# Lightning attention with a bilinear FFN: one kv update in another slot, one scaling on GpSimd, three idle matmuls out

## The chip, the cores and the metric

One core of a Trainium2 chip. The metric is the device time of one execution in microseconds (us); the profile of one execution comes with it, and its span is some 2 us shorter than the device time.

## The reference

Linear attention over blocks with a decay per head, then an FFN whose hidden layer is a product of two projections. Cut to what matters:

```python
for b in range(nb):                       # blocks of the sequence, per batch and head
    intra = einsum(qb, kb) * Dmask        # scores within the block, causal, decayed
    out   = intra @ vb + (qb * lam_pow) @ kv_state
    kv_state = lam_block * kv_state + einsum(kb * rev_pow, vb)
x = out as [B*S, H*D]
result = ((x @ w_a) * (x @ w_b)) @ w_out
```

B, H, S, D are 4, 8, 768, 64. The FFN is 512 to 1536 and back to 512. Inputs and output are f32; the result may carry bf16 error.

## The kernel before

The kernel works in 24 units of 128 tokens, six for each batch. The FFN runs over groups of 4, 1, 2, 4, 4, 4, 4 and 1 units. While TensorE works on the FFN of one group, "hooks" slip in the attention pieces of later units. A table says which piece is recorded at which slot. Each engine executes its own instructions in the order in which they are recorded, and so does the sync engine, from whose queue nearly all transfers are issued.

```python
PLAN = {
    ...
    1: [(0, "V", 4), (2, "T", 5), (3, "PK", 6), (6, "PV", 6), ...],
    2: [(0, "V", 6), (1, "T", 7), (1, "P", 8), (4, "T", 8), (5, "P", 9), (6, "S", 7),
        (6, "S", 8), (7, "V", 7), (8, "P", 10), (10, "T", 9), (11, "T", 10),
        (12, "Q", (7, 8, 9, 10)), (12, "P", 11), (13, "V", 9), (14, "P", 12), ...],
    3: [(3, "S", 11), (3, "S", 12)],
}
for _g, _u in ((3, 11), (4, 15), (5, 19)):
    PLAN.setdefault(_g, []).extend(
        [(1, "P", _u + 2), (3, "P", _u + 3), (4, "V", _u),
         (7, "Q", (_u, _u + 1, _u + 2, _u + 3)), ...])
```

P prepares a unit: q and k are scaled by powers of the decay into `qk` (its half PK), v is cast to `vb`, and loads of later units are issued (its half PV). T transposes q and k on TensorE. From unit 11 on there is no T: a DMA transpose does it, issued as soon as q and k are scaled. S makes scores and masks. V makes the kv update and its copy to SBUF. Q makes the outputs of two units and the scores of the next two.

```python
    def prep_k(u):
        early = u < n0 + 3                               # n0 = 4
        make_ks(u, "dve" if early else "pool")
        make_qs(u, "pool")
        used["u"] = u + 1
        if u >= DMA_T_FROM:                              # 11
            ...
            nc.sync.dma_start_transpose(out=qkT..., in_=U[u]["qk"]...)

    def prep_v(u):
        make_vb(u, "pool" if u < n0 + 3 else "dve")
        pump()                                           # loads up to unit used + 2

    def pieces_O(us, nxt=()):                            # pieces O, O2 and Q
        kqs = [score_banks() for u in nxt]
        for u in us:
            inter(u)                                     # needs the state of unit u - 1
        for u, kq in zip(nxt, kqs):
            scores(u, kq)
        for u in us:
            intra(u)
            evac_o(u, ...)
        if len(us) == 2 and us[0] >= n0 + 3:
            kv_beside(us[1])                             # eight 64-column matmuls
        for u, kq in zip(nxt, kqs):
            masks(u, kq)                                 # two VectorE ops per unit
        if len(us) == 2 and us[0] >= n0 + 3 and us[1] % NB < NB - 1:
            kv_copy(us[1], kv["ps"])

    # head
    for at, i, j in ((2, 0, 0), (3, 0, 1), (4, 1, 0)):
        scale4("k", i, j)
        part_k(i, j, at)
        warm(3)                                          # three idle matmuls of 128 columns
    scale4("k", 1, 1)
```

Of the kernel before, what the change touches and what calls it, by code (L numbers as in the profile page):

```python
# [22 lines left out]
def _bc(ap, dims):  # L23
# [20 lines left out]
    1: [(0, "V", 4), (2, "T", 5), (3, "PK", 6), (6, "PV", 6), (6, "S", 5), (7, "T", 6),  # L44
        (10, "S", 6), (12, "O2", (5, 6)), (13, "P", 7)],
    2: [(0, "V", 6), (1, "T", 7), (1, "P", 8), (4, "T", 8), (5, "P", 9), (6, "S", 7),
        (6, "S", 8), (7, "V", 7), (8, "P", 10), (10, "T", 9), (11, "T", 10),
        (12, "Q", (7, 8, 9, 10)), (12, "P", 11), (13, "V", 9), (14, "P", 12),
        (14, "O2", (9, 10))],
    3: [(3, "S", 11), (3, "S", 12)],  # L50
# [12 lines left out]
def kernel(  # L63
# [12 lines left out]
    B, H, S, D = q.shape  # L76
    BLK = 128
    NB = S // BLK
# [89 lines left out]
    n0 = GROUPS[0]  # L168
# [24 lines left out]
    def warm(n, cols=128):  # L193
        for _ in range(n):
            nc.tensor.matmul(idle_ps[:, :cols], lhsT=idle_sb[:, :128], rhs=idle_sb[:, :cols],  # L195
                             start=True, stop=True, skip_group_check=True)
# [55 lines left out]
    def eng_of(name):  # L252
        return nc.gpsimd if name == "pool" else nc.vector

    def make_ks(u, eng):
        qk = prep_pool.tile([128, 2, H, D], BF16, name="qk", tag="qk")
        eng_of(eng).tensor_mul(qk[:, 1], raw.pop((u, "k")),  # L257
                               lp_k[:, u % NB].to_broadcast([128, H, D]))
        U[u] = dict(qk=qk, kn=qk[:, 1])

    def make_qs(u, eng):
        eng_of(eng).tensor_mul(U[u]["qk"][:, 0], raw.pop((u, "q")),  # L262
                               lp_q[:, u % NB].to_broadcast([128, H, D]))
# [8 lines left out]
        U[u]["vb"] = vb  # L272

    def prep_k(u):
        early = u < n0 + 3
        make_ks(u, "dve" if early else "pool")
        make_qs(u, "pool")
        used["u"] = u + 1
        if u >= DMA_T_FROM:
            qkT = qkT_pool.tile([128, 2, HP, 128], BF16, name="qkT", tag="qkT")  # L280
            nc.sync.dma_start_transpose(
                out=qkT[:].rearrange("p j hp i -> p (j hp) i"),
                in_=U[u]["qk"][:].rearrange("p j h d -> p (j h d)"))
            U[u]["qT"], U[u]["kT"] = qkT[:, 0], qkT[:, 1]
# [15 lines left out]
    def score_banks():  # L300
        return [ps_bank(f"kq{i}", [128, HP, 128], F32) for i in range(2)]

    def scores(u, kq=None):
        d = U[u]
        kq = kq or score_banks()
        for hp in range(HP):
            for i in range(2):
                p = slice(64 * i, 64 * i + 64)
                nc.tensor.matmul(kq[i][:, hp, :], lhsT=d["kT"][p, hp, :], rhs=d["qT"][p, hp, :],  # L309
                                 start=True, stop=True, skip_group_check=True)  # L310
        return kq

    def masks(u, kq):
        ms = mask(kq)
        U[u]["m"] = lambda i, hp: ms[i][:, hp, :]
# [15 lines left out]
    def inter(u):  # L331
        d = U[u]
        if u % NB > 0:
            first = o_bank(u)
            for hp in range(HP):
                nc.tensor.matmul(d["o"][:, hp, :], lhsT=st_bufs[(u - 1) % 4][:, hp, :, :],  # L336
                                 rhs=d["qT"][:, hp, :], start=(first and hp == 0), stop=True,
                                 skip_group_check=True)

    def intra(u, first=False):  # L340
        d = U[u]
        first = o_bank(u) or first
        for hp in range(HP):
            for i in range(2):
                p = slice(64 * i, 64 * i + 64)
                nc.tensor.matmul(d["o"][p, hp, :], lhsT=d["vb"][:, 2 * hp + i, :],  # L346
                                 rhs=d["m"](i, hp), start=(first and hp == 0),
                                 stop=True, skip_group_check=True)

    def evac_o(u, xT, col, eng="act"):  # L350
        o_ps = U[u].pop("o")
        if eng == "act":
            nc.scalar.copy(xT[:, :, col:col + BLK], o_ps)  # L353
        else:
            nc.vector.tensor_copy(xT[:, :, col:col + BLK], o_ps)
# [19 lines left out]
    def kv_beside(u):  # L375
        if u % NB == 0 or u % NB == NB - 1:
            kv_update(u)
        for hp in range(HP if 0 < u % NB < NB - 1 else 0):
            for i in range(2):
                p = slice(64 * i, 64 * i + 64)  # L380
                nc.tensor.matmul(kv["ps"][p, hp, i, :], lhsT=U[u]["kn"][:, 2 * hp + i, :],
                                 rhs=U[u]["vb"][:, 2 * hp + i, :],
                                 start=False, stop=True, skip_group_check=True)

    def kv_copy(u, ps, eng="dve"):
        st = st_bufs[u % 4]
        if eng == "act":
            for i in range(2):
                p = slice(64 * i, 64 * i + 64)
                nc.scalar.copy(st[p, :, i, :], ps[p, :, i, :])  # L390
        else:
            nc.vector.tensor_mul(st[:].rearrange("p hp i d -> p hp (i d)"),  # L392
                                 ps[:].rearrange("p hp i d -> p hp (i d)"), bdiag_bc)
# [11 lines left out]
    def pieces_O(us, nxt=()):  # L405
        kqs = [score_banks() for u in nxt]
        for u in us:
            inter(u)
# [3 lines that stand above are left out]
            intra(u)  # L412
            xT, col = xTs[u]
            evac_o(u, xT, col)
        if len(us) == 2 and us[0] >= n0 + 3:
            kv_beside(us[1])
        for u, kq in zip(nxt, kqs):
            masks(u, kq)
        if len(us) == 2 and us[0] >= n0 + 3 and us[1] % NB < NB - 1:
            kv_copy(us[1], kv["ps"])  # L420


# [89 lines left out]
    def scale4(w, i, j):  # L512
        hs = slice(4 * i + 2 * j, 4 * i + 2 * j + 2)
        nc.vector.tensor_mul(
            xs4[w].rearrange("p r (h d) -> p h r d", d=D)[:, hs],
            x4[w, i][:, :, 2 * j:2 * j + 2].rearrange("p r h d -> p h r d"),
            (lp_q if w == "q" else lp_k)[:, NB:, hs, :].rearrange("p r h o -> p h r o")
            .to_broadcast([128, 2, PACK, D]))
        if j == 1:
            staged.pop((w + "4", i))  # L520
# [9 lines left out]
    def part_k(i, j, at):  # L530
        tps = packed_bank("k", at)
        transpose4("k", i, j, tps)
        unpack(i, tps, slice(j, j + 1), "k")
# [45 lines left out]
    for at, i, j in ((2, 0, 0), (3, 0, 1), (4, 1, 0)):  # L579
        scale4("k", i, j)  # L580
        part_k(i, j, at)
        warm(3)
    scale4("k", 1, 1)
    for u in range(n0):
        make_vb(u, "pool")
# [39 lines left out]
    for g, n in enumerate(GROUPS):  # L625
# [6 lines left out]
        def hook(slot, plan=plan):  # L632
            for name, us in plan.get(slot, ()):
                if name == "C":
                    cast_w("o", us, "dve")
                elif name == "PK":
                    prep_k(us)
                elif name == "PV":
                    prep_v(us)
                elif name == "P":  # L640
                    prep_k(us)
                    prep_v(us)
                elif name == "T":
                    piece_T(us)
                elif name == "S":
                    piece_S(us)
                elif name == "V":
                    piece_V(us)
                elif name == "O":
                    pieces_O((us,))  # L650
                elif name == "O2":
                    pieces_O(us)
                else:
                    pieces_O(us[:2], us[2:])
# [31 lines left out]
```

## Time and profile before

| | before |
|---|---|
| device time, median of the first three executions | 236.69 us (236.5 to 237.27) |
| the profiled execution | 236.32 us, span 234.5 us |
| TensorE busy | 226.2 us |

The prediction shows the lines that carry the argument. In the timeline, the columns are start, duration, engine, source line, operation, tiles and shapes; brackets give the engine's idle time just before and what ended it. In the chain of waits, a piece has start, duration and what ran or was waited for. In a list of waits, the figures are total us, number of waits and the longest. The tile names: `a_ps` and `b_ps` are the two projections, `ab` their product, `op` the output projection, `kq` scores, `m` masked scores, `o_ps` attention output, `kvd` and `st` the state in PSUM and SBUF, `tps` and `qkT` transposed q and k.

The view of tile qkT, for this one transfer, gives the time from issue to landing:

```profile
DMA to landing us min/median/max: 6.2/6.2/6.2
```

So it lands at 94.87 + 6.2 = 101.07. The sixteen score matmuls take 0.55 us gapless (100.94 to 101.49), so those of unit 14, the second eight, start near 101.21. The profile lists no wait here, and the margin is some 0.14 us, an estimate, as the time to landing is given to 0.1 us only.

### The profile page before, as it was taken

The page shows a single profiled execution, that of the slowest core. Times are in us where ns is not written, and L with a number is a line of the kernel's source. Part 1 is how long each engine was busy: PE and PEld are TensorE (multiplying, and loading weights), DVE is VectorE, ACT ScalarE, POOL GpSimd, SP SyncE. Part 2 cuts the span into 40 slices and gives each one's busy share as a digit, 9 for nine tenths or more (in the row PEclk, how much of TensorE's full clock was granted, in tenths as well). Part 3 has the DMA queues.
Part 4 walks back from the last instruction along what each step waited for, and adds up shares of the span by engine and source line. Part 5 has one row for each costly group of instructions (what it writes and reads, how often), then busy time and mean ns, then how long its engine had stood idle before and what let it go on. Part 6 is the DMA issues. An engine that isn't in the chain of part 4 may idle for free.

```text
span 234.5 us, 4593 instructions
## 1 busy us (share of the span) xinstructions
PE 226.2 (96%) x1798; PEld 125.8 (54%) x1798; DVE 115.6 (49%) x205; ACT 92.9 (40%) x174; POOL 48.6 (21%) x63
## 2 busy tenths in 40 slices
PE   7699999999999899999999999999999999999994
PEld 2474444459688554454544454544454544444493
DVE  0896557637459644874144574135574224332050
ACT  3576753066463532242143242242341233431161
POOL 6041000254345453130333330030300000000000
PEclk9999999999999999999999999999999999999999
DMA  4999999999999999999819959515040220000311
GB/s 155 300 285 348 347 366 289 295 213 272 230 244 187 224 198 250 210 161 240 177 48 219 184 73 238 143 64 115 0 48 0 89 87 7 0 3 3 131 48 45
DMA packets 94278, 38.31 MB, mean 163 GB/s; under 512 B 81201, under 2 KB 89777, under 8 KB 94257
## 3 DMA queue, kind: packets, MB, share of 16 engines
q1 hardware_dynamic: 94112, 38.02, 72.1%
q8 instruction: 14, 0.23, 0.4%
q14 instruction: 8, 0.06, 0.1%
q10 hardware_dynamic: 144, 0.00, 0.0%
HBM read 28.32 MB, written 6.29 MB: 148 GB/s over the span
## 4 chain that ended last, share of the span: by engine, by line
PE 90%; DMA 3%; ACT 3%; DVE 2%; issue 1%; SPq 1%; DVEq 0%; ACTq 0%
PE a_ps L428 27%; PE b_ps L428 26%; PE op L449 26%; DMA k<-in_k_dram 3%; PE kq L309 2%; PE o_ps L346 2%; PE o_ps L336 2%; PE kvd L360 1%; PE tps L295 1%; ACT xT L353 1%; ACT o_sb L444 1%; DVE m L321 1%; SPq L207 1%; ACT st L390 1%; PE kq L561 1%
## 5 line engine op out<-in xcount | busy, mean ns | idle before, releaser
L440 DVE TENSOR_TENSOR ab<-a_sb,b_ps 128x512 bf16<-128x512 bf16 (+2 forms) x96 | 52.6, 553 | 80.6 <-PE b_ps L428 58.6
L428 PE MATMUL a_ps<-xT,wa_sb 128*128 128x512 bf16 (+2 forms) x384 | 77.1, 326 | 0.9 <-ACT xT L353 0.6
L428 PE MATMUL b_ps<-xT,wb_sb 128*128 128x512 bf16 (+2 forms) x384 | 77.2, 326 | 0.0
L435 ACT CAST a_sb<-a_ps 128x512 bf16<-128x512 f32 (+2 forms) x96 | 45.6, 481 | 63.5 <-PE a_ps L428 62.0
L449 PE MATMUL op<-wo_sb,ab 128*128 128x512 bf16 (+2 forms) x312 | 65.6, 363 | 0.0
L428 PEld LDWEIGHTS <-wb_sb 128*128 128x128 bf16 x384 | 34.5, 98 | 28.7
L428 PEld LDWEIGHTS <-wa_sb 128*128 128x128 bf16 x384 | 33.8, 98 | 29.4 <-issue 0.9
L449 PEld LDWEIGHTS <-ab 128*128 128x128 bf16 x312 | 28.7, 98 | 29.8
L321 DVE TENSOR_TENSOR m<-kq,lotri 128x512 bf16<-128x512 f32 x48 | 29.9, 683 | 19.3 <-PE kq L309 18.8
L257 POOL TENSOR_TENSOR qk<-kf,lp_k 128x512 bf16<-128x512 f32 x17 | 18.0, 1061 | 77.5 <-issue 31.6
L444 ACT COPY o_sb<-op 128x512 f32<-128x512 f32 (+2 forms) x26 | 14.2, 554 | 37.9 <-PE op L449 37.9
L262 POOL TENSOR_TENSOR qk<-qf,lp_q 128x512 bf16<-128x512 f32 x20 | 21.7, 1083 | 23.0 <-DMA qf<-in_q_dram 23.0
L353 ACT CAST xT<-o_ps 128x512 bf16<-128x512 f32 x23 | 12.5, 590 | 17.5 <-PE o_ps L346 17.4
L392 DVE TENSOR_TENSOR st<-kvd,bdiag 128x512 bf16<-128x512 f32 x18 | 12.3, 684 | 4.9 <-PE kvd L360 3.8
L297 ACT COPY qkT<-tps 128x1024 bf16<-128x1024 bf16 x7 | 7.1, 1012 | 10.4 <-PE tps L295 10.4
L195 PE MATMUL idle<-idle_sb 128*128 128x128 bf16 (+1 forms) x34 | 7.2, 348 | 1.3 <-DVE idle_sb L190 1.3
L271 DVE CAST vb<-vf 128x512 bf16<-128x512 f32 x17 | 8.3, 490 | 0.0
L271 POOL CAST vb<-vf 128x512 bf16<-128x512 f32 x7 | 4.8, 681 | 16.0 <-DMA vf<-in_v_dram 16.0
L346 PE MATMUL o_ps<-m,vb 128*64 128x128 bf16 x192 | 7.9, 222 | 0.0
L336 PEld LDWEIGHTS <-st 128*128 128x128 bf16 x80 | 5.4, 98 | 2.8
L309 PE MATMUL kq<-qkT 64*128 64x128 bf16 x160 | 6.6, 218 | 0.0
L346 PEld LDWEIGHTS <-vb 128*64 128x64 bf16 x192 | 5.8, 109 | 1.4
(54 smaller groups left out, 84.0 us busy)
## 6 DMA issues: line engine op xcount, KB each, us to landing
vf<-in_v_dram SPq DMA_DIRECT2D x24, 256.0 KB, 5.0
out_dram<-o_sb SPq DMA_DIRECT2D x23, 256.0 KB, 2.2
qf<-in_q_dram SPq DMA_DIRECT2D x20, 256.0 KB, 4.7
kf<-in_k_dram SPq DMA_DIRECT2D x20, 256.0 KB, 5.1
wst<-in_moe_w_a_dram SPq DMA_DIRECT2D x6, 512.0 KB, 8.7
wst<-in_moe_w_b_dram SPq DMA_DIRECT2D x6, 512.0 KB, 8.8
wst<-in_moe_w_out_dram SPq DMA_DIRECT2D x6, 512.0 KB, 8.5
q<-in_q_dram SPq DMA_DIRECT2D x2, 512.0 KB, 5.5
```

The costliest lines, as they stand in the source:

```text
L257: eng_of(eng).tensor_mul(qk[:, 1], raw.pop((u, "k")), lp_k[:, u % NB].to_broadcast([128, H, D]))
L262: eng_of(eng).tensor_mul(U[u]["qk"][:, 0], raw.pop((u, "q")), lp_q[:, u % NB].to_broadcast([128, H, D]))
L271: eng_of(eng).tensor_copy(vb, vf)
L321: nc.vector.tensor_mul(m, kq[i], lotri_bc)
L346: nc.tensor.matmul(d["o"][p, hp, :], lhsT=d["vb"][:, 2 * hp + i, :], rhs=d["m"](i, hp), start=(first and hp == 0), stop=True, skip_group_c ...
L353: nc.scalar.copy(xT[:, :, col:col + BLK], o_ps)
L392: nc.vector.tensor_mul(st[:].rearrange("p hp i d -> p hp (i d)"), ps[:].rearrange("p hp i d -> p hp (i d)"), bdiag_bc)
L428: nc.tensor.matmul(ps[:, :gt], lhsT=w_sb[:, s, f * 128:(f + 1) * 128], rhs=xT[:, s, :gt], start=(s == 0), stop=(s == KS - 1))
L435: nc.scalar.copy(a_sb[:, :gt], ps[:, :gt])
L440: nc.vector.tensor_mul(ab[:, f, :gt], a_sb[:, :gt], ps[:, :gt])
L444: nc.scalar.copy(o_sb[:, lo:hi], op[:, lo:hi])
L449: nc.tensor.matmul(op[:, lo:hi], lhsT=ab[:, f, t * 128:(t + 1) * 128], rhs=wo_sb[:, f, lo:hi], start=(f == 0), stop=(f == FC - 1))
```

## The change

The intent is to remove two waits of TensorE on VectorE and some idle work. Unit 8's kv update leaves the piece Q and is recorded two slots earlier, right after unit 9's transposes, so that its copy doesn't stand behind four masks. Unit 6's k is scaled on GpSimd. The third group of idle matmuls in the head goes.

```diff
-        (6, "S", 8), (7, "V", 7), (8, "P", 10), (10, "T", 9), (11, "T", 10),
+        (6, "S", 8), (7, "V", 7), (8, "P", 10), (10, "T", 9), (10, "V", 8), (11, "T", 10),
...
-        early = u < n0 + 3
-        make_ks(u, "dve" if early else "pool")
+        make_ks(u, "dve" if u < n0 + 2 else "pool")
...
-        if len(us) == 2 and us[0] >= n0 + 3:
+        if len(us) == 2 and us[0] >= n0 + 5:
             kv_beside(us[1])
...
-        if len(us) == 2 and us[0] >= n0 + 3 and us[1] % NB < NB - 1:
+        if len(us) == 2 and us[0] >= n0 + 5 and us[1] % NB < NB - 1:
             kv_copy(us[1], kv["ps"])
...
         part_k(i, j, at)
-        warm(3)
+        if i == 0:
+            warm(3)
```

## The prediction

> **What bounds the kernel now.** I read the page's busy line first, then the chain of work that ended last in order of time, then the waits of TensorE, and last the timeline around each break. The page:
>
> ```profile
> PE 226.2 (96%) x1798; PEld 125.8 (54%) x1798; DVE 115.6 (49%) x205; ACT 92.9 (40%) x174; POOL 48.6 (21%) x63
> PEclk9999999999999999999999999999999999999999
> PE 90%; DMA 3%; ACT 3%; DVE 2%; issue 1%; SPq 1%; DVEq 0%; ACTq 0%
> ```
>
> TensorE is busy 96% of the 234.5 us span, it makes up 90% of the chain, and its clock is granted in full throughout. No other engine passes 49%. So time can only come from matmuls left out or from gaps on TensorE, and the gaps are few. The waits of TensorE give all of them that a semaphore explains:
>
> ```profile
> PE kvd L360 <- DVE st L392: 0.9, 1, 0.9
> ...
> PE a_ps L428 <- DVE ab L440: 0.3, 1, 0.3
> ```
>
> These are two single events, and the change aims at both. The chain in order of time shows where they lie. First the short group of one unit (128 tokens), where unit 6's k is scaled:
>
> ```profile
> 55.34 0.04 DVE ab L440
> ...
> 55.54 0.40 DVE qk L257
> ...
> 56.14 0.29 DVE ab L440
> 56.44 0.04 issue
> 56.48 0.38 PE a_ps L428 x4
> ```
>
> Here the chain leaves TensorE for VectorE: the scaling of k (qk) stands in VectorE's queue ahead of an `ab` product, and the first-layer matmul at 56.48 waits for that product, which frees its PSUM bank. Then the second break, some 25 us later:
>
> ```profile
> 79.56 0.35 DVE m L321
> ...
> 80.16 1.28 DVE m L321 x2
> 81.44 0.61 DVE st L392
> ...
> 82.09 0.38 PE kvd L360 x4
> 82.47 1.29 PE op L449 x6
> ```
>
> The timeline has the same place with its releaser:
>
> ```profile
> 81.36 0.68 DVE L392 TENSOR_TENSOR st<-kvd,bdiag 128x512 bf16<-128x512 f32 x1
> 82.09 0.38 PE L360 MATMUL kvd<-vb,qk 128*128 128x128 bf16 x4 [0.85 <-DVE st L392]
> ```
>
> Unit 9's kv matmuls add to the PSUM bank kvd. Unit 8's state copy (st), which reads that bank, stands in VectorE's queue behind four masks (m) of units 9 and 10. TensorE is idle 0.85 us. Between the breaks, and from 86 us to the end, the chain is TensorE nearly without a gap, so a microsecond won before 83 us should arrive at the end in full.
>
> **What the Trainium skill says.** "TensorE: Matmul & The Clock Gate", section Back-to-back issue gap, gives about N/2.4 + 2.5 ns when warm: 56 ns for 128 columns. The chain agrees: eight transposes take 0.45 us, 56 ns each. Its section What's actually happening says that busy TensorE keeps the full clock and idle TensorE can lose it; this matters for leaving out idle matmuls. The clock row above shows no throttling, and no run yet shows the removal. "GPSIMD Engine Reference", section Engine selection, calls GpSimd about twice as slow for two-input elementwise work. Here it is 1043 ns against 682 ns for the same scaling of k, so 1.5 times. The same page, section Specifications, says that the SBUF interface is shared with VectorE, with contention when a VectorE instruction has two SBUF inputs. The trace agrees in the one place it can: GpSimd's scaling took 1.26 instead of 1.04 us at 55.87, alongside VectorE's scaling at 55.54.
>
> **The change, part by part.** The order of the built programs, with the PSUM bank given to each tile, shows the same rotation of the seven banks in both; kvd has a bank of its own, so nothing shifts there.
>
> (a) *Unit 8's kv update.* Before, it ran as eight 64-column matmuls after unit 8's output, with its copy behind the masks. Now it is four 128-column matmuls right after unit 9's transposes, with the copy before the last `ab` of that group. The cost of the stall, from starts: the half output block before it starts at 79.77; another such block of six, at 61.80, has its follower at 63.11, 1.31 us later. Unit 9's kv matmuls would then start at 81.08 and take 0.22, as a gapless kv update at 72.04 does, so the next block would start at 81.30 instead of 82.31: 1.01 us won. That is more than the 0.85 of idle, as a restarted matmul queue also pays its fill (0.38 against 0.22 in the chain). Against it: four matmuls of 56 ns are 0.22 us, the eight removed ones took 0.12 in the chain (two column halves run side by side), so 0.10 is added. Net -0.91.
>
> Does the moved copy hurt where it lands? At the slot, kvd is free (unit 7's copy ended at 74.93) and v of unit 8 was cast at 65.69. VectorE has a backlog there until about 76.65; the copy takes 0.68 and pushes the last `ab` from 76.89 to about 77.2, ended by 77.6. Its bank is wanted by the first state matmul (o_ps), at 77.98 before and about 78.20 now: half a microsecond in hand. Then VectorE was idle 1.65 us before the masks, so this work moves into idle time.
>
> (b) *Unit 6's k on GpSimd.* VectorE loses one 0.68 us op. The `ab` that released TensorE at 56.44 then ends near 55.9, before the score matmuls in front are through. What TensorE gains, again from starts: unit 5's scores start at 55.81 and the following b_ps at 56.70, 0.89 later; the gapless twin for unit 6 is 58.84 to 59.40, 0.56. So -0.33. GpSimd pays 1.04 us more. k of unit 6 was issued at 46.69; with the median 5.3 us to landing it is there at about 52.0. Two scalings end near 54.1, v of unit 6 follows to about 54.7, and unit 7's k comes only at 55.87, bound by its load. The transposes of unit 6 are at 56.86, over 2 us later. Hidden.
>
> (c) *Three idle matmuls in the head.* The chain has them in line at 11.47 for 0.17 us. The scores behind them need copies ended by 11.20, so they can start at once and no gap opens to cool the clock. But the head ends in a meeting of two chains: the first a_ps waits for ScalarE (evacuation over at about 18.68) while its weights wait for GpSimd's cast, over at about 18.38 after a load that TensorE cannot hasten; the weight load of 18.67 is put down to that cast. If that is right nearly nothing is won, if ScalarE was the last, 0.17. I take 0.10.
>
> Sum: 0.91 + 0.33 + 0.10 = 1.34 us of 236.69, so 235.3 us, 0.6% less.
>
> **The rivals.** First: the wait is replaced by another. Unit 10's state matmuls need unit 9's copy. VectorE leaves the masks at about 81.6 (before 81.36, plus 0.22 for the added matmuls), casts one v (0.34), and copies unit 9's state to about 82.6. TensorE, no longer stalled, wants this state as weights at about 82.7 to 82.9. The margin is 0.1 to 0.3 us where it was about 0.8. If it is missed, TensorE waits on st in o_ps instead; I would expect 0.1 to 0.3 lost and 235.5. For it speaks the thin margin; against it that all terms are taken from durations repeating to a few hundredths.
>
> Second: the loads set the pace, so that TensorE arrives earlier and waits. GpSimd does wait 23 us for q and 11 us for k by load. Against it: q and k of units 7 to 10 are scaled at 58.1, 64.3, 68.2 and 72.2, and their transposes come at 65.1, 68.1, 74.9 and 76.2, so at least 3.9 us in hand against 1.3 won; from 86 us on TensorE had no idle in its 35.40 us stretch. If some stage did hold, the gain would be 0.3 to 0.9 smaller, and the time near 236.
>
> Third: VectorE becomes the bound around the moved copy, because four masks of units 7 and 8 and two casts crowd it. TensorE did lose some 0.2 us there at 74.05, behind those masks, but that is ahead of the new copy. If `ab` came too late anyway, 0.3 would go: 235.6.
>
> Fourth, on the better side: GpSimd's scaling of unit 12's k waited 3.1 us for unit 8's kv matmuls (at 79.98) and comes about 4 us earlier, which brings the DMA transpose after it forward. Its reader at 93.8 was not waiting, so I expect nothing.
>
> **Range and chances.** The terms give 1.34; everything in part (c) and no rival gives 1.41, and a shorter wait elsewhere in the crowded group might add 0.2; the rivals together take off up to 0.9. Before's own three runs lie within 0.77 us, which matters more than these: from 235.3 I allow -0.6 and +0.9, so 234.7 to 236.2. Faster by over 2% would need less than 231.96, 4.7 us, and the removable waits do not hold that much; slower by over 2%, over 241.4, would need a new stall several times larger than any TensorE has now. Each gets 1%.
>
> **What would show it.** (a) right: no wait of kvd on st near 81 us, the group of 256 tokens about 0.9 us shorter, eight fewer matmuls of 64 columns and four more of 128. Wrong: a wait of o_ps or its weights on st, or of o_ps on `ab`. (b) right: the 0.3 wait of a_ps on `ab` gone, one scaling of k less on VectorE and one more on GpSimd, transposes of unit 6 without a wait. (c) right: the first a_ps at about 18.6 instead of 18.73; wrong: the same start, with the cast as releaser; badly wrong: digits under 9 in the clock row. The whole is wrong if the gap reopens after 86 us: waits on q, k or v where TensorE had none.

## More of the kernel before

The transposed q and k of unit 14 are issued here by the sync engine's queue (SPq), and the scores of units 13 and 14 follow on TensorE:

```profile
94.87 2.20 SPq L281 DMA_TRANSPOSE qkT<-qk  x1
...
100.94 0.62 PE L309 MATMUL kq<-qkT 64*128 64x128 bf16 x16
```

## The result, and the profile after

| | before | after |
|---|---|---|
| median of six executions | 236.56 us (236.32 to 237.27) | 236.19 us (235.86 to 236.58) |
| ratio | | 0.9981, 95% interval 0.9964 to 0.9998 |
| profiled execution, span | 234.5 us | 234.8 us |

A ratio is the mean time of one kernel's fast runs over that of the other's of the same rounds, so it is not quite the ratio of the medians. The gain is about 0.2%, some 0.4 us, a third of the 1.34 predicted. The two profiled executions flatter the kernel before: 236.32 us is the fastest of its six, and 236.58 us the slowest of the six after.

In the profile after, both waits that the change aimed at are gone. This is the list of TensorE's waits, from its top and with one line left out at the end:

```profile
PE kq L308 <- DMA qkT<-qk: 1.7, 1, 1.7
PE tq L524 <- DVE scratch L513: 1.5, 4, 0.9
PE idle L195 <- DVE idle_sb L190: 1.3, 1, 1.3
PE tk L524 <- DVE scratch L513: 0.7, 2, 0.4
PE a_ps L427 <- ACT xT L352: 0.6, 2, 0.5
```

The first line is new: scores wait 1.7 us for a DMA transpose. Where was the gain until then? These are the starts of the four-unit group that begins near 86 us, in the timeline of TensorE; first before, then after:

```profile
86.15 1.03 PE L428 MATMUL a_ps<-xT,wa_sb 128*128 128x512 bf16 x4
```

```profile
84.49 1.03 PE L427 MATMUL a_ps<-xT,wa_sb 128*128 128x512 bf16 x4
```

TensorE is there 1.66 us earlier, more than predicted. Further on in the same view, after:

```profile
98.97 0.39 PE L335 MATMUL o_ps<-qkT,st 128*128 128x128 bf16 x4
99.28 0.40 PE L308 MATMUL kq<-qkT 64*128 64x128 bf16 x8
101.42 0.40 PE L308 MATMUL kq<-qkT 64*128 64x128 bf16 x8 [1.74 <-DMA qkT<-qk]
```

Unit 13's scores start 1.66 us earlier than before, at 99.28 for 100.94. Unit 14's start at 101.42, where before they started near 101.21. All of the gain is gone within this one wait, and from here to the end both traces run in step, 0.26 us apart the wrong way. The chain of waits after says what it was:

```profile
94.76 0.27 SPq L126
...
95.14 6.23 DMA qkT<-qk
101.37 0.05 issue
101.42 0.40 PE kq L308 x8
```

The transpose of unit 14 was issued at 95.14 (94.87 before) and took 6.23 us. The transfers did not move with TensorE. The theory, called A in what follows: in this stretch the DMA work keeps its own pace, it brings unit 14's q and k at about 101.1 to 101.8 us whatever TensorE does, and the kernel before already stood at this limit. Rival B: the change itself slowed the queue, for GpSimd now scales unit 6's k and frees load buffers later. Rival C: TensorE became slower after 86 us for another reason.

### The profile page after: what moved, and what is told of

It is laid out like the page before. It is cut to its first block, busy times and chain, and to the rows that moved or that the text cites. A ratio compares the mean times of both kernels' runs of the same rounds, so it can differ in the third digit from the quotient of the medians.

```text
span 234.8 us, 4577 instructions
## 1 busy us (share of the span) xinstructions
PE 225.4 (96%) x1791; PEld 125.4 (53%) x1791; DVE 114.5 (49%) x204; ACT 93.0 (40%) x174; POOL 48.7 (21%) x64
## 4 chain that ended last, share of the span: by engine, by line
PE 87%; DMA 6%; ACT 2%; DVE 1%; SPq 1%; issue 1%; DVEq 0%; ACTq 0%
PE op L448 26%; PE a_ps L427 26%; PE b_ps L427 25%; DMA k<-in_k_dram 3%; DMA qkT<-qk 3%; PE o_ps L345 2%; PE kq L308 2%; PE o_ps L335 1%; PE kvd L359 1%; PE tps L294 1%; DVE m L320 1%; ACT xT L352 1%; ACT o_sb L443 1%; SPq L207 1%; ACT st L389 1%
## 5 line engine op out<-in xcount | busy, mean ns | idle before, releaser
L257 POOL TENSOR_TENSOR qk<-kf,lp_k 128x512 bf16<-128x512 f32 x18 | 19.0, 1058 | 79.6 <-PE kvd L359 31.2
L262 POOL TENSOR_TENSOR qk<-qf,lp_q 128x512 bf16<-128x512 f32 x20 | 21.0, 1048 | 23.2 <-DMA qf<-in_q_dram 23.2
L195 PE MATMUL idle<-idle_sb 128*128 128x128 bf16 (+1 forms) x31 | 6.4, 344 | 1.3 <-DVE idle_sb L190 1.3
L271 DVE CAST vb<-vf 128x512 bf16<-128x512 f32 x17 | 7.6, 449 | 0.0
L308 PEld LDWEIGHTS <-qkT 64*128 64x128 bf16 x160 | 4.5, 94 | 3.9 <-DMA qkT<-qk 1.9
```

Source lines behind the costliest of these rows:

```text
L257: eng_of(eng).tensor_mul(qk[:, 1], raw.pop((u, "k")), lp_k[:, u % NB].to_broadcast([128, H, D]))
L262: eng_of(eng).tensor_mul(U[u]["qk"][:, 0], raw.pop((u, "q")), lp_q[:, u % NB].to_broadcast([128, H, D]))
L308: nc.tensor.matmul(kq[i][:, hp, :], lhsT=d["kT"][p, hp, :], rhs=d["qT"][p, hp, :], start=True, stop=True, skip_group_check=True)
```

## The experiments

Three sets of four kernels ran, each set on one chip with the kernel before among them. The medians of the kernel before were 236.76, 236.65 and 236.85 us there. "Wait" is TensorE's wait for the transpose of unit 14 in the profiled execution; a dash means that its list of waits has none.

| kernel | median us (six runs) | ratio to before, interval | wait |
|---|---|---|---|
| after_t14 | 234.64 (234.61 to 234.67) | 0.9893 (0.9851 to 0.9935) | - |
| before_t14 | 236.06 (235.99 to 236.12) | 0.9953 (0.9906 to 1.0) | - |
| a_alone | 236.46 (235.72 to 236.99) | 0.9969 (0.9925 to 1.0014) | 1.0 |
| after_idle | 236.47 (235.81 to 236.92) | 0.9965 (0.9921 to 1.0009) | 1.1 |
| bt14_a | 235.25 (235.12 to 235.29) | 0.9941 (0.9921 to 0.9961) | - |
| bt14_b | 235.67 (235.64 to 235.74) | 0.996 (0.9942 to 0.9978) | - |
| bt14_c | 236.13 (235.82 to 236.5) | 0.998 (0.9961 to 1.0) | - |
| bt14_idle | 237.18 (237.11 to 239.77) | 1.0041 (1.0006 to 1.0076) | - |
| v_contig, wrong result | 235.14 (234.55 to 235.28) | 0.9906 (0.9872 to 0.9941) | - |
| stores_act | 235.94 (235.64 to 236.15) | 0.9944 (0.9907 to 0.9981) | 1.5 |
| after_again | 236.6 (235.32 to 238.04) | 0.998 (0.9935 to 1.0026) | 1.6 |
| bt14_c_act | 235.95 (235.77 to 236.72) | 0.9951 (0.9916 to 0.9985) | - |

All but v_contig gave correct results.

### after_t14 and before_t14: the transpose first

Unit 14's q and k are scaled, and their transpose recorded, before the loads of unit 16; once in the changed kernel, once in the kernel before.

```diff
     PLAN.setdefault(_g, []).extend(
-        [(1, "P", _u + 2), (3, "P", _u + 3), (4, "V", _u),
+        ([(1, "PK", 13), (1, "PK", 14), (1, "PV", 13), (3, "PV", 14)] if _g == 3 else
+         [(1, "P", _u + 2), (3, "P", _u + 3)]) + [(4, "V", _u),
```

> The changed kernel with the DMA transpose of unit 14 put ahead of the loads of unit 16 in the DMA queue. Theory A (the saturated, in-order DMA queue delivers unit 14's transposed q and k at about 101.4 us whatever TensorE does, and the kernel before was already within about 0.2 us of that): the 1.7 us wait of the scores on this transpose goes, and the gain of 1.66 us that stands at the start of the four-unit group (84.49 against 86.15) arrives at the end: 235.0 us, ratio to before 0.993 to 0.994. Theory B (the change slowed the DMA queue itself by moving unit 6's k to GpSimd, so the delay is the change's own): the transpose still comes earlier, so about the same, but then the same edit also gives the kernel before nothing to lose. Theory C (TensorE is slower after 86 us for another reason): ratio stays near 0.998.

> The same move of unit 14's transpose in the kernel before. Theory A: nothing waits for this transpose there, so ratio 0.999 to 1.001 (at most 0.1 us). If the move itself were worth a microsecond for another reason (for instance less contention), this would be near 0.995, and the run with the changed kernel would prove nothing.

The changed kernel fell to 234.64 us, below the 235.0 expected. Its sync engine issues both transposes together, and the scores run without a gap; two views of after_t14:

```profile
90.94 3.00 SPq L281 DMA_TRANSPOSE qkT<-qk  x2
```

```profile
99.34 0.62 PE L309 MATMUL kq<-qkT 64*128 64x128 bf16 x16
99.89 0.64 PE L346 MATMUL o_ps<-m,vb 128*64 128x128 bf16 x16
```

Against the kernel before with the same edit, on the same chip, the three parts are worth 236.06 - 234.64 = 1.42 us. (The 1.66 us between the first two traces is more, as some 0.2 us of it go with a slow cast in before, 0.82 us for 0.42, that before_t14 did not have; see bt14_c below.) Theory C falls: once the transpose is early, the gain arrives at the end.

The expectation for before_t14 was a miss. It should have gained nothing and gained 0.7 us by the medians (the interval just touches 1.0). But look at the spreads. The kernel before ran from 236.03 to 239.52 in that set, and with the transpose early from 235.99 to 236.12; its best run is as fast as the new median. So the kernel before probably also loses to this transfer in many executions, and the profiled one, at 236.32 us, was one of its faster ones, in which the transfer happened to come 0.14 us before it was needed. For this speaks that the best runs differ by 0.04 us only. It is not shown: no execution of the kernel before that waits for the transfer was profiled. Of the 0.26 us between the two profiled executions, 0.18 stand already in the scores of unit 13 (100.94 and 100.76), ahead of any need of the transfer. These go with the slow cast, so the transfer is not the only source of the difference.

### a_alone: one part, with the transpose where it was

```diff
-        (6, "S", 8), (7, "V", 7), (8, "P", 10), (10, "T", 9), (11, "T", 10),
+        (6, "S", 8), (7, "V", 7), (8, "P", 10), (10, "T", 9), (10, "V", 8), (11, "T", 10),
-        if len(us) == 2 and us[0] >= n0 + 3 ...          # both places
+        if len(us) == 2 and us[0] >= n0 + 5 ...
```

> Only unit 8's kv update moved. TensorE should reach the four-unit group about 0.9 to 1.1 us earlier than before (85.0 to 85.2 against 86.15). Theory A: the scores of unit 14 then wait about 0.8 to 1.0 us for the transpose and the whole gains only 0.1 to 0.5 us, ratio 0.998 to 0.9995, as much as all three parts together. Theory B: without the move of unit 6's k the DMA queue is not slowed, and the full 0.9 us arrives: ratio 0.996.

The trace of a_alone:

```profile
85.05 1.03 PE L428 MATMUL a_ps<-xT,wa_sb 128*128 128x512 bf16 x3
...
101.25 0.40 PE L309 MATMUL kq<-qkT 64*128 64x128 bf16 x8 [1.02 <-DMA qkT<-qk]
```

(The first of the four matmuls is in a row of its own, some 0.2 us earlier.) The transpose was issued at 94.97 and landed 6.2 us later. Unit 6's k stays on VectorE here, and the transfer still comes at 101.2, so rival B isn't needed. The wait is shorter just because TensorE is less early. The time does not decide: 0.9969 lies between what the two theories expected, and its interval holds both. The trace does.

### after_idle and bt14_idle: work put into the wait

Five idle matmuls of 512 columns, 1.08 us, ahead of the scores; once in the changed kernel and once in the kernel before with the transpose early.

```diff
         ps = ps_bank(name, [128, 512], F32, ffn=True)
+        for _ in range(5 if name == "a_ps" and f == 6 and used["u"] == 15 else 0):
+            nc.tensor.matmul(ps, lhsT=idle_sb[:, :128], rhs=idle_sb, start=True, stop=True, ...)
```

> The changed kernel with five idle matmuls of 512 columns (5 x 0.216 = 1.08 us of TensorE) in the four-unit group ahead of the scores that wait for unit 14's transpose. Theory A: they fill the wait, which shrinks from 1.7 to about 0.65 us, and the time stays that of the changed kernel, ratio to before 0.998 (0.997 to 0.999). If TensorE's own work set the pace there, it would be 1.08 us longer: ratio 1.002 to 1.003.

> The same base with the five idle matmuls (1.08 us) ahead of the scores. With the transpose early TensorE sets the pace, so all of it must show: 237.1 us. Theory A stands on this contrast: in the changed kernel, where the transpose was late, the same matmuls cost 0.3 us at most. If it shows less than 0.5 us here, something else than TensorE sets the pace of this group in this kernel too.

In the changed kernel the 1.08 us cost 0.28 by the medians of two sets (236.19 and 236.47), inside the spread of both. In the kernel with the transpose early they cost 1.12 (236.06 and 237.18, again two sets, but both tight; one run of 239.77 aside), and in its traces the scores of unit 13 move from 100.76 to 101.84, by 1.08. The wait in after_idle:

```profile
101.86 0.40 PE L308 MATMUL kq<-qkT 64*128 64x128 bf16 x8 [1.05 <-DMA qkT<-qk]
```

It shrank by 0.69 rather than 1.08, as the transfer landed 0.4 us later in this execution (issued at 95.99, 5.8 us to landing). The idle matmuls can't have delayed it: they start at 95.56, and unit 13's transpose was already late, at 91.93 for 91.17. This is the plainest evidence for theory A: by the medians some 0.8 of the 1.08 us was free, because TensorE waited there.

### bt14_a, bt14_b, bt14_c: the three terms by themselves

Each part alone, on the kernel before with the transpose early.

```diff
bt14_a, as in a_alone:
+        ... (10, "T", 9), (10, "V", 8), (11, "T", 10),
+        if len(us) == 2 and us[0] >= n0 + 5 ...
bt14_b:
-        make_ks(u, "dve" if early else "pool")
+        make_ks(u, "dve" if u < n0 + 2 else "pool")
bt14_c:
-        warm(3)
+        if i == 0:
+            warm(3)
```

> The kernel before with unit 14's transpose early, plus part (a) alone, the move of unit 8's kv update. With the wait on the transpose out of the way (236.06 us without any part), the term is seen by itself: predicted 0.91, the trace of the changed kernel suggests up to 1.1 with the second-order effect. Theory A: 235.0 to 235.15. If (a) depends on (b) for its gain: 235.4 or more.

> The same base plus part (b) alone, unit 6's k on GpSimd. Predicted 0.33: 235.73. In the trace of the changed kernel a second wait near 74 us went too (0.2 us), because a cast on VectorE no longer ran beside a GpSimd scaling (0.42 instead of 0.82 us). If that comes from (b): 235.5.

> The same base plus part (c) alone, three idle matmuls left out. Predicted 0.10, from a range of 0 to 0.17; the trace of the changed kernel shows the first first-layer matmul 0.18 us earlier. So 235.88 to 236.0. If the cast on GpSimd held the head, 236.06.

The base was not run in this set, but bt14_idle less its 1.08 us is 236.10, next to the 236.06 of the other chip. So (a) is worth 0.81 (predicted 0.91; its 235.25 us missed the expected range by 0.1), (b) 0.39 (predicted 0.33), and (c) nothing that can be seen: -0.07, with a spread of 0.68 us against 0.17 and 0.10 in the other two. The three add up to 1.13 of the 1.42 that they are worth together; no run tells where the other 0.29 comes from, though the 0.15 by which after_t14 starts the FFN earlier (18.61 for 18.76) would be part of it. Yet TensorE does start the FFN earlier; bt14_a has the head as before, bt14_c without the matmuls:

```profile
18.77 1.02 PE L429 MATMUL a_ps<-xT,wa_sb 128*128 128x512 bf16 x3 [0.45 <-ACT xT L354]
```

```profile
18.63 1.24 PE L429 MATMUL a_ps<-xT,wa_sb 128*128 128x512 bf16 x4 [0.45 <-ACT xT L354]
```

These 0.14 us are lost again between 70 and 86 us, and more: the scores of unit 13 start 0.28 us later than in before_t14 (101.04 for 100.76). VectorE and GpSimd there, in bt14_c:

```profile
70.35 0.98 DVE L272 CAST vb<-vf 128x512 bf16<-128x512 f32 x1
71.25 0.41 DVE L441 TENSOR_TENSOR ab<-a_sb,b_ps 128x256 bf16<-128x256 bf16 x1
71.58 2.47 DVE L322 TENSOR_TENSOR m<-kq,lotri 128x512 bf16<-128x512 f32 x4
```

```profile
70.00 1.04 POOL L258 TENSOR_TENSOR qk<-kf,lp_k 128x512 bf16<-128x512 f32 x1 [2.09 <-PE a_ps L429]
71.00 1.23 POOL L263 TENSOR_TENSOR qk<-qf,lp_q 128x512 bf16<-128x512 f32 x1
```

The cast of v takes 0.98 us while GpSimd scales. It stands in front of the masks, and TensorE ran into a short stall behind them. The same thing divides before from after, in the cast of v of unit 9; before first:

```profile
70.45 0.82 DVE L271 CAST vb<-vf 128x512 bf16<-128x512 f32 x1
```

```profile
69.92 0.42 DVE L271 CAST vb<-vf 128x512 bf16<-128x512 f32 x1
```

Before, GpSimd was scaling from 69.95 on; after, it began at 70.35, when the cast was over. The Trainium skill, "GPSIMD Engine Reference", section Specifications, names just this contention: with VectorE instructions in a two-port mode or with two SBUF inputs. "VectorE: DVE Perf Modes", section "Mode 2×_2P — use both read ports for one tensor", lists copies from SBUF as such instructions. The traces agree: in before and in bt14_c such a cast took 0.42 us alone, and 0.81 to 1.18 us beside a scaling. Since the scaling starts when a load lands, which of the two an execution gets is a matter of some tenths of a microsecond.

### bt14_c_act: is it the casts?

```diff
-        make_vb(u, "pool" if u < n0 + 3 else "dve")
+        make_vb(u, "act" if u in (9, 10) else "pool" if u < n0 + 3 else "dve")
```

> Part (c) alone with the transpose early, and the casts of v of units 9 and 10 on ScalarE instead of VectorE. In the profiled run of part (c) those casts took 0.98 and 1.18 us beside GpSimd's scalings, against 0.42 alone, and TensorE lost some 0.3 us behind them. If that hid the gain of (c), the time is now 235.7 to 235.95 and its six runs lie within 0.2 us (236.13 and 0.68 before). If the spread has another cause it stays.

The median came to 235.95 and five of six runs lie within 0.26 us; one is at 236.72. In the profiled run the scores of unit 13 start at 100.65, against 100.76 in before_t14: 0.11 earlier. This points to some 0.1 us for (c), and fits the casts, but one outlier and another chip leave it unsettled.

### v_contig and stores_act: what sets the pace of the transfers

In v_contig the loads of v of units 8 to 16 take the same bytes from long runs of memory (wrong values). In stores_act the two output stores between the loads and the transpose are issued by ScalarE.

```diff
+        if w == "v" and 8 <= u <= 16:
+            src = v[b].rearrange("h s d -> (h s d)").rearrange(
+                "(n p h d) -> n p h d", p=128, h=H, d=D)[nb]
```

```diff
+        eng = nc.scalar if row in (5, 6) else nc.sync
+        eng.dma_start(out=out_r[row][:, lo:hi], in_=o_sb[:, lo:hi])
```

> Wrong results on purpose: the changed kernel with v of units 8 to 16 loaded from 2 KB runs of memory instead of 256 B runs, the same bytes in an eighth of the packets. If the DMA engines' work on small packets sets when unit 14's transpose comes through, it is issued and lands at least 1.5 us earlier, the wait goes, and the time is that of the changed kernel with the transpose early: 234.6 to 235.0 us. If the pace is the queue's own issuing, one transfer at a time whatever its size, it stays at 236.2.

> The changed kernel with the two output stores of units 5 and 6, which stand between the loads and unit 14's transpose in the sync engine's queue, issued from ScalarE. If the sync engine's issue time is what delays the transpose, it comes about 2 us earlier (two stores of about 1 us) and the time falls to 234.8 to 235.2. If the DMA engines are what is full, the two stores take their share all the same, the transpose lands less than 0.5 us earlier, and the time stays above 235.7.

The issue of unit 14's transpose in v_contig, then in stores_act:

```profile
92.64 1.52 SPq L284 DMA_TRANSPOSE qkT<-qk  x1
```

```profile
95.31 2.12 SPq L280 DMA_TRANSPOSE qkT<-qk  x1
```

With fewer and larger packets it goes out 2.5 us earlier than in the changed kernel, lands in 4.3 us, and the wait is gone. So the work on small packets sets the pace: between 63 and 101 us, 29,338 of 29,727 packets in the changed kernel are under 512 B. (The profiled execution of v_contig, at 234.55 us, was the fastest of its six.)

What this work fills first, the DMA engines, the sync engine's issuing or the window of eight told of below, stays open. stores_act was to tell the first two apart. With two stores fewer ahead of it the transpose goes out no earlier (95.31 for 95.14), lands at 101.2, and TensorE waits 1.5 us. But the edit brought a new wait with it. The sync engine's longest wait between 84 and 96 us in stores_act:

```profile
SPq L126 <- DMA out_dram<-o_sb: 1.6, 1, 1.6
```

In the built program each transfer also waits for the one eight places before it. The load of v that went out at 88.78 in the changed kernel had one of the moved stores eight places before it here; that store was issued at 85.36 and took 5.1 us, so the load went out at 90.52. This took most of the 2.15 us of issuing that the edit had freed (1.00 and 1.15), so the run does not decide about the issuing. The Trainium skill, "Perfetto Trace Analysis", section What "DMA-bound" means, names the DMA engines and the issuing sequencer as two different bounds and says that larger descriptors help with both. Larger packets did help here. Both signs are there in the changed kernel: the sync engine's track is solid from 74 to 110 us, and the busy row of the DMA engines, 63 to 101 us, is full nearly throughout:

```profile
DMA  9899999999497999999996999999999999999909
```

v_contig ended at 235.14, 0.1 above the range expected; why it isn't at 234.64 is open.

### after_again: the changed kernel once more

No edit.

> The changed kernel once more, on the same chip as these: 236.0 to 236.4 us with a spread of over 0.4 us, as its end depends on when a transfer lands; against 0.06 us of spread where the transpose is early.

236.6 us, and the spread is wider than expected: 2.7 us over six executions. Its profile shows the same wait, 1.6 us. The ratio, 0.998, repeats the first result.

## Why the prediction was right or wrong

- **What bounds the kernel, the chain.** Right as far as the profile went, wrong in one inference: "so a microsecond won before 83 us should arrive at the end in full". It was won (1.66 us at the start of the next group) and didn't arrive.
- **(a), the kv update.** Right. Predicted 0.91, measured 0.81 by itself. One term of its sum was misread: the eight removed matmuls did not take 0.12. That is the chain's piece for unit 10's; from starts, as the rest of the sum is counted, they took 0.22 (79.55 to 79.77), as long as the four that replace them. The wait of kvd on st is gone, and no wait of o_ps on st or on `ab` took its place, so the first and the third rival didn't occur. The fourth was half right: GpSimd scaled unit 12's k 1.7 us earlier (78.29 for 79.98), not 4, and the transpose after it went out no earlier (85.81 for 85.42).
- **(b), the scaling.** Right. Predicted 0.33, measured 0.39.
- **(c), the idle matmuls.** The head ended 0.18 us earlier in the profiled execution (18.73 to 18.55), more than the 0.10 taken. This repeats: the first a_ps starts at 18.73 to 18.77 in the six profiles with the matmuls, and at 18.54 to 18.64 in the eight without. By the time (c) could not be separated from noise. The clock was granted in full after it (1.0 in the profiled run). Of the two chains that meet there, ScalarE's seems to be the one that counts: in bt14_c the first a_ps starts at 18.63, though GpSimd's cast ends at 18.82 (spans on GpSimd are rough).
- **What it took from the skill.** The Trainium skill, "TensorE: Matmul & The Clock Gate", section Back-to-back issue gap, gives N/2.4 + 2.5 ns for a single isolated matmul, and some 81 ns at 128 columns for a stream of weight loads and matmuls. The eight transposes are such a stream and took 56 ns each, so the measurement decides for the 56. And the row on SBUF that the prediction took from "GPSIMD Engine Reference", section Specifications, also names VectorE's two-port modes. The prediction left these out, so "the one place it can" wasn't: in the same profile a cast of v took 0.82 us beside a scaling at 70.45. Durations did not all repeat "to a few hundredths".
- **The sum.** 1.34 predicted, 1.42 measured, where nothing else held it up (after_t14 against before_t14).
- **The step that failed** is the second rival, "the loads set the pace". It was dismissed with two arguments. The first gave the margin of units 7 to 10, "at least 3.9 us in hand"; those were the wrong units, as their transposes run on TensorE. The second was that "from 86 us on TensorE had no idle in its 35.40 us stretch". An absent wait isn't a margin: for unit 14 the lines of the trace give 101.07 for the landing and 101.21 for the need. So TensorE, 1.66 us early, waited 1.74 us for this transpose, which was issued at 95.14 for 94.87, no earlier than before. The fourth rival stopped at unit 12's reader "at 93.8" and did not follow the queue to unit 14. The size put on the second rival, a loss of "0.3 to 0.9", was about right: 0.9 of 1.34 was lost by the time measured, and it happened as a matter of course: all five profiles with part (a), the loads of before and the transpose in its old place show the wait, 1.0 to 1.7 us.
- **The spread.** "Before's own three runs lie within 0.77 us" was read as noise of the measurement. It was a hint: with the transpose early, the six runs of before_t14 lie within 0.13 us. But it isn't the only source of spread: also with the transpose early, the runs of bt14_c spread over 0.68 us, and one of bt14_idle was 2.6 us off.
- **Range and chances.** The chances of a change over 2% rested on the sizes of the waits and held. The range ends at 236.2 and the median came to 236.19, which is luck: the upper end had been put there for the rivals and the spread, and another set gave 236.6 for the same kernel.

## What to carry to other kernels

Before a gain on the busy engine is carried through to the end, follow each transfer that feeds it later and write down landing and need, also where the profile lists no wait; the smallest of these margins caps the gain. A spread of some tenths of a per cent in an otherwise repeatable kernel can mean that one transfer and one engine arrive nearly together. Here the cure cost nothing: the transfer needed first went ahead of loads needed later, and with it the change is worth 1.4 us instead of 0.4, at 234.64 us the fastest correct kernel.

## What the Trainium skill lacked or had wrong

- "Perfetto Trace Analysis", section What "DMA-bound" means: it takes a solid track of the issuing engine as the sign of a bound by the sequencer. Here that track was solid from 74 to 110 us while the DMA engines' busy row was full too, so the sign alone did not decide. Larger descriptors, which the page advises for both, were tried in v_contig and brought the transpose from 95.14 to 92.64.
- "GPSIMD Engine Reference", section Engine selection: about twice as slow for two inputs; here 1.04 us against 0.68, 1.5 times.
- "DMA: Bandwidth & Descriptors": it has no time from issue to landing for a DMA transpose under load. Here the same 128x1024 transpose took 3.0 to 6.6 us.
- No page that bears on this says that a list of waits shows no margins: some 0.14 us of margin stood behind a stretch without any wait, and capped a gain of 1.4 us.
